# Second group of an FFN given three-pass products in its second layer, with late weight differences and one pair of attention blocks moved

## The chip, the cores and the metric

The kernel runs on one core of one Trainium2 chip. The metric is the device time of one execution in microseconds (us); the number to beat is the median of three timed runs, 521.12 us (521.03 to 521.21). A separate execution was profiled; its times are those of the profile below. The engines are called as the profile calls them: PE (matrix products), PEld (PE's loads of the stationary operand, which run beside its products), DVE (VectorE), ACT (ScalarE), POOL (GpSimd) and SP (SyncE, which only issues transfers here).

## The reference

The computation is gated linear attention followed by a two-layer FFN. All inputs are 64-bit floats on the host.

```
q, k, v: (4, 8, 768, 48)      alpha: (4, 8, 768, 48), between 0.8 and 1
for t in range(768):
    state = alpha[:, :, t, :, None] * state + einsum('bhd,bhe->bhde', k[:, :, t], v[:, :, t])
    y[:, :, t] = einsum('bhd,bhde->bhe', q[:, :, t], state)
x = y.transpose(0, 2, 1, 3).reshape(3072, 384)
h = maximum(x @ w_in, 0)           # w_in (384, 2048)
out = (h * h) @ w_out              # w_out (2048, 384)
```

The attention inputs reach the kernel as 32-bit floats. The weights reach it as 64-bit words, which DVE and ACT turn into fp32 by bit operations (`convert_first` to `convert_second`, from L154).

## The kernel before, in words

**Blocks and groups.** The sequence is cut into 6 chunks of 128 tokens. A chunk of one of the 4 batches is a block, so there are 24 blocks, and attention works on pairs of blocks (the pair that begins with block n is called pair n). Four blocks, 512 tokens, make a group of the FFN. There are 6 groups, 0 to 5 in the code; the text calls them group 0 to group 5, so "the second group" of the title is group 1 and "the third" is group 2. While the PE runs the FFN of one group, the attention of the next group's two pairs is worked in between.

**First layer.** The 2048 hidden rows are 16 tiles of 128 rows, two tiles to each of 8 pieces of the weights (a piece of `w_in` is 128x768 numbers, and so is a piece of `w_out`). A tile is 3 products of 128x128 by 128x512 per pass, since the model dimension is 3x128. The result is squared after a ReLU on ACT and DVE (`in_post`).

**Second layer.** Each hidden tile is multiplied, for each of the 4 token blocks t, with a 128x384 slice of `w_out`, and the 16 tiles are summed in one PSUM bank per block.

**Two ways to multiply.** A plain fp32 product (`out_plain`, `ffn_in`) is one matmul, which the trace shows as two records. The other way is three passes in a faster type (fp32r). The weight w becomes b, a rounded copy of 0.9998 w (`cast_w`, ACT), l, the rest w - b divided by 2^-12 (`rest_w` on DVE and `scale_w` on ACT), and d = b - l (`diff_w`, DVE). The data becomes a, l and d in the same manner (`split_to`, `diff_to`: a on ACT, l and d on DVE, once for each 128x512 tile). The product is (1 + E)(a b + l l) + d d with E = 2^-12. In the profile the passes carry the operands' names: `wb,xa`, `wl,xl`, `wd,xd` in the first layer, `wb,ha` (or `hx`), `wl,hl` (or `hx`), `wd,hd` in the second. `out_x` does the first two passes of a hidden tile, and `out_y` does the third afterwards, two pieces at a time.

**Which group uses which way.** Group 0: first layer plain; second layer plain for pieces 0 to 5 and three passes for 6 and 7 (`k0` = 2). Group 1: first layer in three passes; second layer plain for pieces 0 to 3 and three passes for 4 to 7 (`k1` = 4). Groups 2 to 5: everything in three passes.

**Where the parts live.** The parts are made once, by `prepare`, during groups 0 and 1. b stays in the core's memory. l and d are stored to DRAM as they are made (`keep`) and come back in each later group as that group needs them: `stream` puts their keys in the list `todo`, and `pump` (L699) issues the loads in that order while fewer than `room` buffers are in use; `used` frees a buffer after its last product and calls `pump`. In group 1 the parts needed in that group are kept instead of loaded (`diff_w`).

**What sets the order.** Each engine works its instructions in the order in which the program emits them. That order is written out: a layer is a list of units with a cost in PE time, and all the rest (attention, conversions, preparation, splits of x) are events with a time on the same scale. `weave` walks the units, adds up their costs and emits an event when the sum reaches its time. The table `AT` (L19) holds these times: `g1` and `g` say when the pairs of the next group begin, `g1x`, `gx` and `g0x` when the next group's x is split, `w_first`, `o0`, `o2` and `w_in_at` when parts of the weights are prepared. In `attention`, `joined`, `ga` and `gb` finish an older pair's outputs (with the copies `x<-y` at L628 that write the next group's x), and `turn` (matmuls at L590) transposes q and k of the pair that begins. SP issues all transfers in one order, and a transfer that has to wait (for instance a store of a part not yet made) holds all those behind it.

**Alignment.** `align` (L1016) asks for the PE's next instruction to lie at a given offset from a 256-byte boundary of the program. It is filled with empty instructions, which are the NOPs of L1018 in the profile. `places` and `pads` in `AT` say where. Before the change there are 5 such places, with 58, 26, 26, 26 and 22 NOPs.

**Lines of the profile.** L737 is the first layer's three passes, L930 the plain first layer, L820 every product of the second layer, L710 ACT's casts to a, L660 DVE's rests l and also `diff_w`'s and `in_y`'s sums, L714 DVE's differences d of the data, L754 and L752 ACT's work after the first layer, L628 the copies of y into x, L412 the matmuls of y, L490 the attention state's update.

## Time and profile before

| what | number |
|---|---|
| median of 3 runs | 521.12 us (521.03 to 521.21) |
| profiled execution | 521.61 us, of which the span that the trace covers is 519.8 us |
| busy: PE, PEld, DVE, ACT | 511.1, 421.5, 361.9, 316.4 us |
| granted PE clock | 1.00 in every stretch |
| plain products of the second layer (160 records), groups 0 and 1 | 53.5 us |
| third pass of the second layer (304) | 53.7 us |
| group 1, first product to group 2's first | 126.26 to 214.62 us |
| group 2, the same way | 214.62 to 295.75 us |

The span lacks the time around the execution: 521.61 - 519.8 = 1.8 us. The mean duration of a product overstates its cost, since products overlap at their ends; what one costs is found by dividing a stretch of back-to-back products by their number. Busy time of PE is near the whole span, so the profile has to be read by stretches of time, and by the idle time just ahead of a product, which the trace gives in square brackets together with what ended it.

### The profile page before, as it was taken

How to read it: one execution, taken by the hardware profiler on the slowest of the kernel's cores; microseconds unless marked ns; L12 is line 12 of the kernel's file. 1: busy time of each engine (PE TensorE's matmuls, PEld its weight loads, DVE VectorE, ACT ScalarE, POOL GpSimd, SP SyncE). 2: the span in 40 equal slices, each digit the busy share in tenths (PEclk: the TensorE clock that was granted, in tenths of full speed). 3: DMA queues.
4: the chain of work that ended last, by engine and by line, in shares of the span. 5: the costliest groups of instructions: out<-in, count | busy, mean ns of one | idle time of the engine just before them, and what ended most of it. 6: DMA issues, size and time to landing. Idle time of an engine off the chain costs nothing.

```text
span 519.8 us, 13204 instructions
## 1 busy us (share of the span) xinstructions
PE 511.1 (98%) x5350; PEld 421.5 (81%) x5350; DVE 361.9 (70%) x629; ACT 316.4 (61%) x664; POOL 5.4 (1%) x29
## 2 busy tenths in 40 slices
PE   8989999999999999999999999999999999999997
PEld 6775446668887669888899988899988899988997
DVE  3887969998979579757596466696465485363861
ACT  5678893687899566476963266962266863164620
POOL 4000000000000000000000000000000000000000
PEclk9999999999999999999999999999999999999999
DMA  9999686517878496998885796965684534798101
GB/s 182 210 262 262 178 216 172 75 51 240 243 228 200 117 280 161 272 338 234 201 235 156 242 269 185 231 172 162 217 269 124 183 123 153 254 355 295 68 0 62
DMA packets 139324, 102.36 MB, mean 197 GB/s; under 512 B 109808, under 2 KB 112896, under 8 KB 139264
## 3 DMA queue, kind: packets, MB, share of 16 engines
q1 hardware_dynamic: 139264, 101.52, 68.6%
q8 instruction: 43, 0.70, 0.6%
q14 instruction: 17, 0.14, 0.1%
HBM read 84.17 MB, written 17.33 MB: 195 GB/s over the span
## 4 chain that ended last, share of the span: by engine, by line
PE 93%; DVE 3%; DMA 1%; SPq 1%; issue 1%; ACT 0%; DVEq 0%; POOLq 0%
PE o L820 41%; PE h L737 32%; PE h L930 8%; PE y L412 4%; PE T L590 2%; PE sckv L432 2%; PE sckv L460 2%; DVE x L628 1%; DMA a_in<-in_alpha_dram 1%; PE cs L297 1%; SPq L344 1%; DMA last<-row 1%; PE cs L301 1%; PE cs L300 1%; SPq L119 0%
## 5 line engine op out<-in xcount | busy, mean ns | idle before, releaser
L737 PE MATMUL h<-xa,wb 128*128 128x512 f32 x240 | 69.2, 396 | 1.2 <-PE h L737 0.8
L737 PE MATMUL h<-xl,wl 128*128 128x512 f32 x240 | 68.1, 392 | 0.0
L737 PE MATMUL h<-xd,wd 128*128 128x512 f32 x240 | 66.6, 393 | 0.0
L754 ACT ACTIVATE h<-h 128x512 f32<-128x512 f32 x40 | 23.3, 581 | 57.9 <-PE h L737 57.7
L660 DVE TENSOR_TENSOR hid<-h,hid 128x512 f32<-128x512 f32 x40 | 27.5, 688 | 42.1 <-PE h L737 39.3
L628 ACT COPY x<-y 32x256 f32<-32x256 f32 (+2 forms) x132 | 47.2, 365 | 15.7 <-PE y L412 13.2
L820 PE MATMUL o<-wb,ha 128*128 128x384 f32 x160 | 54.2, 339 | 0.0
L820 PE MATMUL o<-wd,hd 128*128 128x384 f32 x304 | 53.7, 334 | 0.0
L820 PE MATMUL o<-w_out,hid 128*128 128x384 f32 x160 | 53.5, 490 | 0.0
L820 PE MATMUL o<-wl,hl 128*128 128x384 f32 x160 | 53.5, 334 | 0.0
L737 PEld LDWEIGHTS h<-xl,wl 128*128 128x128 f32 x240 | 44.9, 188 | 10.6 <-ACT wl L679 0.6
L737 PEld LDWEIGHTS h<-xa,wb 128*128 128x128 f32 x240 | 44.2, 188 | 11.1 <-PE h L737 1.2
L820 PEld LDWEIGHTS o<-wd,hd 128*128 128x128 f32 x304 | 52.8, 188 | 0.0
L737 PEld LDWEIGHTS h<-xd,wd 128*128 128x128 f32 x240 | 44.5, 188 | 9.2 <-ACT hid L752 0.2
L820 PE MATMUL o<-wb,hx 128*128 128x384 f32 x144 | 48.7, 338 | 0.0
L820 PE MATMUL o<-wl,hx 128*128 128x384 f32 x144 | 48.1, 334 | 0.0
L820 PEld LDWEIGHTS o<-w_out,hid 128*128 128x128 f32 x160 | 29.9, 190 | 19.7
L930 PE MATMUL h<-x,w_in 128*128 128x512 f32 (+1 forms) x120 | 43.0, 510 | 1.5 <-DVE s L489 1.2
L710 ACT ACTIVATE ha<-hid 128x512 fp32r<-128x512 f32 x40 | 25.4, 636 | 23.8 <-DVE hx L660 12.9
L752 ACT ACTIVATE hid<-h 128x512 f32<-128x512 f32 x40 | 24.3, 607 | 25.1 <-PE h L737 25.0
L930 PEld LDWEIGHTS h<-x,w_in 128*128 128x128 f32 x120 | 22.5, 190 | 18.6 <-issue 14.9
L660 DVE TENSOR_TENSOR hl<-hid,ha 128x512 fp32r<-128x512 f32 x40 | 27.4, 685 | 10.9 <-ACT ha L710 10.8
(115 smaller groups left out, 883.0 us busy)
## 6 DMA issues: line engine op xcount, KB each, us to landing
wd<-do SPq DMA_DIRECT2D x36, 384.0 KB
wl<-lo SPq DMA_DIRECT2D x34, 384.0 KB
wl<-li SPq DMA_DIRECT2D x32, 384.0 KB
wd<-di SPq DMA_DIRECT2D x32, 384.0 KB
raw<-in_moe_w_in_dram SPq DMA_DIRECT2D x8, 768.0 KB
raw<-in_moe_w_out_dram SPq DMA_DIRECT2D x8, 768.0 KB
v_in<-in_v_dram SPq DMA_DIRECT2D x24, 192.0 KB
out_dram<-osb SPq DMA_DIRECT2D x24, 192.0 KB
```

The source lines that it names most:

```text
L412: ins = nc.tensor.matmul(out=ys[e][64 * half : 64 * half + D + G * e, m % 2, p // 2, t], lhsT=lhsT, rhs=rhs, start=(half, e) not in seen, ...
L432: nc.tensor.matmul(out=ps[e][HALF[h], 0, p, :], lhsT=ks[rows, p, HALF[h]], rhs=qs[rows, p, HALF[h]], start=True, stop=True, skip_group_che ...
L460: nc.tensor.matmul(out=ps[h][64 * e : 64 * (e + 1), 1, p, G:64], lhsT=tile_of("k", n)[HALF[h], 2 * p + e, :], rhs=tiles["v"][n % NV][HALF[ ...
L590: nc.tensor.transpose(out=ps[h][:, i, p, :], in_=rows[HALF[h], 128 * p : 128 * (p + 1)], identity=ident[HALF[h], HALF[h]],)
L628: copy(out=x[kk][to : to + m, t : t + 2], in_=blk[n]["y"][e][r : r + m, :, p // 2],)
L660: nc.vector.tensor_tensor(out=o, in0=x, in1=z, op=op)
L710: nc.scalar.activation(out=a, in_=x, func=AF.Copy, scale=NEAR)
L737: nc.tensor.matmul(out=acc["h", j], lhsT=here[w, "i", p][:, kk, jj * 128 : (jj + 1) * 128], rhs=x_parts[x][:, kk], start=start and kk == 0 ...
L752: nc.scalar.activation(out=hid[j], in_=x, func=AF.Copy, scale=E)
L754: nc.scalar.activation(out=x, in_=x, func=AF.Copy, scale=1.0 + E)
L820: nc.tensor.matmul(out=acc[t][:, 0:DM], lhsT=lhs[:, t * C : (t + 1) * C], rhs=rhs, start=start, stop=stop, skip_group_check=True,)
L930: nc.tensor.matmul(out=ps, lhsT=w[:, kk, c0 : c0 + 128], rhs=xT[g][kk][:, cols], start=(kk == 0), stop=(kk == KM - 1),)
```

## The change

- Group 1 works all 8 pieces of the second layer in three passes. The plain path stays for group 0's six pieces only; `k1`, `h1`, `late`, `ffn_out` and `plain_out` go.
- Group 1 takes its pieces in the order 6, 7, 0, 1, 2, 3, 4, 5 in both layers (`pieces`, `tiles_of`, `js`), and `w_in`'s parts are prepared in that order. Group 0 already made the parts of pieces 6 and 7 of `w_out`.
- For the other six pieces of `w_out` (`lasting`), d is made late, all within a short stretch near the end of the second layer's first two passes (`d_at`, `d_by`), and it is written over l in l's own buffer (`here.pop` in `diff_w`). `used` therefore does not free such an l in group 1. The dict `made` goes; its entries are in `here`.
- Signs are turned round (-NEAR, and add in place of subtract). The products are the same: each has two negated factors or none.
- The tile splits at the start of a second layer begin one unit later in group 1 (`lead1` 5), and in every group the later splits are emitted up to 4 tiles ahead instead of 6 (`ahead`). The limit on buffers in group 1 is 23 instead of 22.
- In group 1 the third pair event no longer begins pair 12: it only finishes pair 10's outputs. Pair 12 begins in group 2, whose list `g2` has three entries and whose x splits have their own time (`g2x`).
- The loads of v and k in `attention` move (`v_by`), and so do many times in `AT`.
- `pads` has 11 entries instead of 3. With the two `places` that gives 13 alignments; their NOPs come to 288 instead of 158, by the addresses of the instructions.

In numbers of instructions emitted: PE matmuls 3683 to 3747 (32 plain ones go, 96 passes come), DVE tensor-tensor 347 to 355, DVE scalar-pointer forms 203 to 207, ACT activations 435 to 443, transfers 350 to 348.

The diff, cut; the table's entries are put one to a line:

```diff
 AT = {
-'v_by': (2.5, 3.5, 5.0)
+'v_by': (1.0, 0.87, 13.76)
-'pads': ((1, 33.0, 218), (2, 0.5, 83), (2, 5.5, 178))
+'pads': ((1, 20.0, 24), (1, 26.0, 232), (1, 33.0, 36), (1, 38.0, 111), (1, 43.0, 132),
+         (2, 2.0, 126), (2, 8.0, 248), (2, 13.0, 153), (2, 22.0, 42), (2, 28.0, 11), (2, 36.0, 72))
+'lead1': 5
-'w_first': (45.25, 42.0, 55.95)
+'w_first': (45.63, 40.88, 58.08)
+'d_at': 42.74, 'd_by': 0.4
-'w_late': 0.6, 'w_in_by': 3.4, 'room1': 22, 'ahead': 6
+'w_late': 2.1, 'w_in_by': 3.6, 'room1': 23, 'ahead': 4
-'g0': ((1.5, 4, False, True, 28.25), (20.25, 6, True, True), (28.75, 8, True, False))
+'g0': ((3.5, 4, False, True, 28.38), (21.25, 6, True, True), (27.13, 8, True, False))
-'g1': ((5.5, 8, False, 15.5), (15.5, 10, True), (34.5, 12, True))
+'g1': ((4.87, 8, False, True, 16.12), (15.49, 10, True, True), (32.99, 12, True, False))
+'g2': ((5.0, 12, False, True, 17.63), (15.63, 14, True, True), (35.0, 16, True, True))
-'g1x': 50.0, 'g0x': 55.25
+'g1x': 50.12, 'g2x': 49.99, 'g0x': 55.76
-'k1': 4, 'h1': 3
-'o0': (44.75, 47.25), 'o2': (21.75, 27.5, 31.75, 35.0, 41.25, 41.75), 'str1': 22.0
+'o0': (45.25, 46.87), 'o2': (20.75, 23.25, 27.62, 28.12, 32.24, 34.26), 'str1': 24.12
...
+    def lasting(w, p):
+        return w == "o" and p < NW - AT["k0"]
...
     def diff_w(w, p):
-        b, l = here["b", w, p].bitcast(FP32), made["l", w, p].bitcast(FP32)
-        d = made["d", w, p] = wt("wd", FP32R, shapes[w])
-        cut.add((w, p))
-        combine(((d, b, ALU.subtract, l),))
+        l = here["l", w, p]
+        d = here["d", w, p] = here.pop(("l", w, p)) if lasting(w, p) else wt("wd", FP32R, shapes[w])
+        combine(((d, here["b", w, p].bitcast(FP32), ALU.add, l.bitcast(FP32)),))
         keep("d", w, p)
...
     def pump():
-        while todo and todo[0] in stored and len(here) + len(made) + 2 * NW - len(cut) < room[0]:
+        while todo and todo[0] in stored and len(here) + 2 * NW - len(cut) < room[0]:
...
-    def used(*key):
-        here.pop(key)
+    def used(x, w, p):
+        if g_now[0] != 1 or x != "l" or not lasting(w, p):
+            here.pop((x, w, p))
         pump()
...
+    def pieces(g):
+        last = [*range(NW - AT["k0"], NW)]
+        return last if g == 0 else last + [*range(NW - AT["k0"])] if g == 1 else [*range(NW)]
+
+    def tiles_of(g):
+        return [2 * p + i for p in pieces(g) for i in range(2)]
...
     def layer_out(g):
-        plain = NW - AT["k0"] if g == 0 else NW - AT["k1"] if g == 1 else 0
+        ps, ns = pieces(g), tiles_of(g)
+        plain = NW - len(ps)
...
         if g == 1:
...
+            for i, at in enumerate(AT["o2"]):
+                events += prepare(
+                    at0 + at, "o", order[len(AT["o0"]) + i], 0, at0 + AT["d_at"] + AT["d_by"] * i
+                )
```

## The prediction

> **What bounds the kernel now.** I read first the busy times, then the chain of waits by engine, then a table of stages, then the idle time ahead of single products.

> ```profile
> PE 511.1 (98%) x5350; PEld 421.5 (81%) x5350; DVE 361.9 (70%) x629; ACT 316.4 (61%) x664; POOL 5.4 (1%) x29
> PE 93%; DVE 3%; DMA 1%; SPq 1%; issue 1%; ACT 0%; DVEq 0%; POOLq 0%
> 126.20:168.90 42.70, 42.70 (x506) 34.22 (x504) 37.64 (x68) 37.84 (x77) 0.00 (x0) 1.00 0.76 205
> 168.90:214.60 45.70, 45.70 (x556) 35.85 (x549) 36.13 (x65) 28.14 (x63) 0.00 (x0) 1.00 0.73 202
> 214.60:295.70 81.10, 79.91 (x923) 71.47 (x922) 52.97 (x100) 45.46 (x103) 0.00 (x0) 1.00 0.81 236
> ```

> PE is 98% busy and 93% of the chain: the number of products sets the time, and what else counts is what keeps PE waiting. The last three lines are stretches (length, then PE, PEld, DVE, ACT busy): both layers of group 1, then group 2. The clock is 1.00 in all. In group 1, DVE is at 37.64 of 42.70 and 36.13 of 45.70, 88% and 79%; in group 2 it is at 65%. So group 1, which the change makes shorter for PE and fuller for DVE, is where DVE is nearest to binding.

> ```profile
> 79.75 9.30 PE L820 MATMUL o<-w_out,hid 128*128 128x384 f32 x28
> 88.97 0.46 PE L590 MATMUL T<-ident,k_in 64*128 64x64 f32 x8
> 266.43 29.32 PE o L820 x168
> 126.26 1.08 PE L737 MATMUL h<-xa,wb 128*128 128x512 f32 x3
> 128.08 0.87 PE L737 MATMUL h<-xa,wb 128*128 128x512 f32 x3
> 216.97 0.93 PE L737 MATMUL h<-xa,wb 128*128 128x512 f32 x3 [0.81 <-PE h L737]
> 241.77 0.97 PE L737 MATMUL h<-xa,wb 128*128 128x512 f32 x3 [0.38 <-DVE hid L660]
> 148.57 0.96 DVE L660 TENSOR_TENSOR wd<-wb,wl 128x768 fp32r<-128x768 f32 x1 [2.46 <-ACT wl L679]
> 171.97 0.36 DVE L490 TENSOR_TENSOR s<-s,last 128x192 f32<-128x192 f32 x1 [2.82 <-DMA last<-row]
> L1018 PEldq NOP  x158: 13/13/13, 50.6 to 249.6; - x158
> ```

> Each timeline line is start, length, then what ran; brackets give idle time and releaser.

> **The products.** 28 records of plain products from 79.75 to the next kind at 88.97 take 9.22 us; a product is two records, so it costs 9.22/14 = 0.659. 168 three-pass products follow without a gap in 29.32: 0.1745 each, 0.5235 for three. The change swaps 32 of the first for 96 of the second: 32 x (0.659 - 0.5235) = **-4.3**.

> By the weight loads the sum would differ. PEld's loads of these products last 0.188 in the trace, more than the 0.1745 a product takes, so here they overlap one another. [...] If a three-pass product cost its load, 96 x 0.188 = 18.0 would replace 21.1, a gain of 3.0. The row of 168 back-to-back products decides for 0.1745.

> **Group 0 to group 1.** The first tile's six products take 126.26 to 128.08, 1.82, where six at the in-layer pitch of 0.227 take 1.36: a stall of 0.46 while the last splits of x arrive. The order of the instructions after the change puts y's second half and its copies into x earlier, so I take **-0.45** (between 0 and that).

> **Group 1, first layer.** Tiles are split into a, l and d; a tile's l and d cost DVE 0.685 + 0.692 by duration and about 1.32 back to back with their dependence. Three tiles' splits now lie here: +4.0 for DVE, and three casts of about 0.5, +1.6, for ACT. Lying in DVE's 5.1 idle us of the first stretch, they fit only if the idle time falls at the right places. Before points at which PE takes a buffer or an x cast just in time, the slack in the trace is 0.05 to 0.16 (at 144.50, 148.67, 156.24, 160.02, 161.72, 165.64). DVE's waits in group 1 up to 161 come to 3.8 (0.53, 0.38, 0.43, and the 2.46 shown); these can absorb most. I walked the new order by hand with the rows' pitches: **+1.6**. Bounds: 0 if all waits are absorbed, 3.8 if DVE's waits recur and all the added work is exposed.

> **Group 1, second layer.** The first half was plain and needed no splits; now all 16 tiles are split during it. Up to the last l, DVE has 9.66 us to do from the seventh tile's on, PE 8.33 until it needs it; the lead at the start covers part: **+0.95**, bounds 0 and 2.8 (the wait at 171.97 recurring in it). The six late d cost 6 x 0.87 = 5.2 of DVE (pitch of 128x768), but they end 3.5 to 6 us before the third pass reads them. They take 0 while that holds; if DVE is that much later, they are exposed one for one. Writing d over l makes each wait for l's last product, which is earlier by the order, and for the store of l, also earlier: 0. SP issues two transfers fewer: 0.

> **Group 1 to group 2.** The second tile waits: chain gap 0.80, idle 0.81 shown at 216.97, 0.98 with the pitch. It has two causes, l of the first `w_in` piece landing at about 215, which held PE's sequencer, and 26 NOPs just behind (215.04 to 216.92). That l now comes from the list earlier: **-0.98**. The casts and rests of x for group 2 are ordered later among the copies: +0.55 (bounds 0 and 0.98).

> **Group 2.** The stall of 0.58 at 241 ends a chain through `last<-row`, a transfer that holds DVE. It belongs to a pair's state update, which moves: **-0.58**. But two pairs and a begun third now lie in group 2: DVE has 28 us free there, so only the exposed ends count: **+0.3** (0 to 0.58, one more such chain).

> **Group 2 to group 3.** Pair 14's outputs now end 4.6 us before group 3's first product; 12 copies of y take 4.4 (line at 120.73 below), then come three casts and three rests of x. Between groups 0 and 1 that lead is 5.6 us and cost 0.46. One us less, of work which is serial on ACT and DVE: 0.46 + 1.0 = **+1.5**; 0.5 if the casts interleave with the copies, 2.0 at most by the walk.

> ```profile
> 120.73 4.37 ACT L628 COPY x<-y 32x256 f32<-32x256 f32 x12 [0.51 <-PE y L412]
> 125.12 1.67 ACT L710 ACTIVATE xa<-x 128x512 fp32r<-128x512 f32 x3
> 127.60 1.89 DVE L714 SCALAR_TENSOR_TENSOR xd<-xa,xl 128x512 fp32r<-128x512 f32 x3
> ```

> **The moved pair.** Pair 12's matmuls and copies on PE, about 4.5 us, leave group 1 and enter group 2: 0 on PE. `ahead` 4 emits splits two tiles later in groups 2 to 5; they still lead their products by four tiles of 1.4: 0, bounds -0.3 and +0.5. The new order of v and k loads puts k behind 13 us more: 0, as both are wanted a group later.

> **NOPs.** 26 take 1.88 us of the sequencer, 72 ns each; 130 more are 9.4 us. They cost when PE's queue runs dry, and the runs are of 8 to 44. Four of the five runs before have no gap behind them, and the fifth came after the sequencer had been held. I take 0; the other bound is +2.0, two or three 40-NOP runs (2.9 each) at places where the queue is short. [...]

> **Sum:** -4.3 - 0.45 + 1.6 + 0.95 - 0.98 + 0.55 - 0.58 + 0.3 + 1.5 = -1.4. The profiled execution would go from 521.61 (span 519.8 and 1.8 around it) to 520.2; it stands 0.5 above the median, so on the median 521.12 - 1.4 = **519.7**.

> **The rivals.**
> - *Waits are hidden.* DVE's own waits of 3.8 in group 1 absorb the splits: 521.12 - 4.3 - 0.45 - 0.98 - 0.58 + 1.5 + 0.3 = 516.6. For it: DVE has 5.1 and 9.6 idle us in the two stretches. Against: the small slacks. Chance 0.20.
> - *DVE becomes the bound of group 1* (the other side). By the walk the last split comes 0.5 us late with no idle time on DVE at all, so every microsecond that DVE idles between 126 and 190 passes to PE; the forecast's 1.6 + 0.95 = 2.55 is that 0.5 and 2.05 of idle time. If the waits of before recur, 3.8 and some two fifths of the 2.8 (1.15, the state update being ordered among the last splits), PE loses 0.5 + 4.95 = 5.45, 2.9 more than forecast: 519.7 + 2.9 = 522.6. The change stops gaining from 2.05 + 1.4 = 3.5 us of idle time. For it: 88% and 79% busy with more work in less time, and waits on ACT and on a transfer that nothing in the diff takes away. Against: the state update begins at another time. Chance 0.20.
> - *Handoffs and NOPs eat the gain.* Group 2 to 3 at 2.0, xl at 0.98, one NOP run exposed: 519.7 + 0.5 + 0.43 + 0.5 = 521.1. Chance 0.14.
> - *The loads set the pitch.* The gain of 3.0 in place of 4.3: 519.7 + 1.3 = 521.0. Chance 0.04.

> **How the numbers follow.** The forecast, 519.7, has 0.42 with its own range 518.4 to 520.9. This kernel's runs differ by 0.03%; 0.2%, 1.04 us, is about what a measurement can tell from no change: faster is below 520.08, slower above 522.16. Faster: 0.30 of the forecast's 0.42 and 0.20 of hidden waits, 0.50. Same: the other 0.12, 0.14 and 0.04, and a little of DVE's case, less 0.02 for its tail, 0.28. Slower: DVE's case and that tail, 0.22. The range reaches from the hidden waits to DVE's case, 516.8 to 522.6.

> **What would show it.** After: no `w_out,hid` records past group 0, so 96 records and not 160; `wd,hd` 336. Group 1's second layer without its plain half, the whole group about 81.7 us with pair 12's 4.5 gone (88.4 - 4.3 - 4.5 - 0.45 + 2.55), group 2 near 84.9 (81.1 + 4.5 - 0.98 + 0.55 - 0.58 + 0.3). If waits are right, idle time ahead of `h` products in group 1 released by DVE `hid` or `hl`, 1 to 3 us; if DVE binds, more than 4 us ahead of `ha`, `hl` products with DVE over 95% there. The idle time at the first tile of group 3 should be 1 to 2 us, released by DVE `xl`. An idle time behind `NOP` runs would falsify their 0. A three-pass product off 0.1745 in group 1, or idle time ahead of `wd` products, falsifies the first term or the late differences' cover.

## The result and the profile after

The changed kernel takes 526.99 us (526.55 to 527.69, four runs) against 521.16 (521.03 to 521.81): the ratio is 1.011, with a 95% interval of 1.0093 to 1.0128. The forecast was 519.7, the range 516.8 to 522.6. The profiled execution of the changed kernel took 527.69, with a span of 525.2 against 519.8.

These are the busy times and the chain by engine of the changed kernel, and its stages: both layers of group 1, then groups 2 and 3. A stage line has its length, then the busy time of PE, PEld, DVE and ACT.

```profile
PE 513.2 (98%) x5382; PEld 426.4 (81%) x5382; DVE 370.8 (71%) x641; ACT 319.8 (61%) x672; POOL 5.4 (1%) x29
PE 83%; DVE 7%; ACT 6%; DMA 2%; issue 1%; SPq 0%; POOL 0%; DVEq 0%; ACTq 0%; POOLq 0%
```

```profile
126.60:170.70 44.10, 43.45 (x506) 34.52 (x504) 40.43 (x72) 38.43 (x78) 0.00 (x0) 1.00 0.76 205
170.70:210.00 39.30, 38.48 (x426) 36.71 (x418) 30.44 (x50) 25.55 (x54) 0.00 (x0) 1.00 0.65 212
210.00:299.50 89.50, 86.28 (x1086) 74.66 (x1084) 59.78 (x116) 48.85 (x116) 0.00 (x0) 1.00 0.75 208
299.50:380.30 80.80, 80.60 (x889) 71.36 (x890) 54.94 (x100) 46.23 (x105) 0.00 (x0) 1.00 0.74 210
```

PE's share of the chain has fallen from 93% to 83%, and DVE and ACT together have risen to 13%. Group 1 has become shorter (83.4 us, from 88.4) and group 2 much longer (89.5, from 81.1). The profile says 98% for PE in both kernels. The share of busy time hides what happened, because a product that starts late is drawn long (0.44 us at 188.54 below, where its neighbours take 0.33).

So I set PE's time against its work. Each product gets the pitch at which such products run back to back in the trace (0.1735 to 0.1745 for one of the second layer's passes, 0.2267 for one of the first's, 0.664 for a plain one); what a step from one product to the next takes beyond that is a gap. Gaps above 0.16 us are listed by themselves, and the smaller ones are summed.

| us | before: work, small, listed | after: work, small, listed | difference |
|---|---|---|---|
| up to group 1 | 126.26 | 126.62 | +0.36 |
| group 1 | 85.84, 2.22, 0.29 | 77.41, 3.18, 2.81 | -8.43 +0.96 +2.52 |
| group 2 | 77.41, 2.01, 1.56 | 81.28, 3.27, 4.96 | +3.87 +1.26 +3.40 |
| group 3 | 76.92, 2.30, 0.17 | 76.92, 2.51, 1.31 | +0.21 +1.14 |
| groups 4 and 5 | | | 0.0 |

The work is down by 8.43 - 3.87 = 4.56 us, and the gaps are up by 9.5. That makes +5.3, of the 5.4 by which the spans differ. How much of it is work hangs on the pitch of a plain product. The 64 records that go from group 1 took 20.74 us in three stretches of the kernel before (5.36, 10.13 and 5.25), 0.648 a product and not 0.664; with that the work falls by 4.05 and the small gaps grow by 1.9 in place of 2.43. Of this growth, 1.3 us lie in the steps right behind a listed gap; what the rest is was not worked out. The largest gaps are in group 2. Here are PE's products around two of them, and the NOP runs of the same stretch and of one that follows (number, then first and last start).

```profile
211.19 1.10 PE L741 MATMUL h<-xl,wl 128*128 128x512 f32 x2
212.12 0.86 PE L741 MATMUL h<-xa,wb 128*128 128x512 f32 x3
214.73 0.93 PE L741 MATMUL h<-xa,wb 128*128 128x512 f32 x3 [1.05 <-issue]
224.87 0.93 PE L741 MATMUL h<-xa,wb 128*128 128x512 f32 x3 [0.98 <-ACT inv L312]
232.86 0.93 PE L741 MATMUL h<-xa,wb 128*128 128x512 f32 x3 [0.21 <-issue]
```

```profile
L1003 PEldq NOP  x40: 13/13/13, 211.8 to 214.7; - x40
L1003 PEldq NOP  x40: 13/13/13, 221.9 to 224.8; - x40
L1003 PEldq NOP  x40: 13/13/13, 229.8 to 232.8; - x40
L1003 PEldq NOP  x10: 13/13/13, 259.5 to 260.1; - x10
```

Each of the four gaps (1.22, 1.15, 0.38, and 0.31 at 260.20; 3.06 in all) ends 0.07 us after the last NOP of a run, to the hundredth: 214.66 and 214.73, 224.80 and 224.87, 232.79 and 232.86, 260.13 and 260.20. In the second, the view of waits names ACT, which is only the last semaphore that it sees. The gap of 0.98 in the kernel before also ends so, 216.91 and 216.97.

The other gaps are waits for data. The timeline shows one of the four in group 1's first layer that end with ACT's scaled l of `w_in`, two in its second layer, released by DVE, and the start of group 3, released by the casts and rests of x.

```profile
150.07 0.97 PE L741 MATMUL h<-xl,wl 128*128 128x512 f32 x3 [0.21 <-ACT wl L685]
188.54 0.44 PE L833 MATMUL o<-wl,hx 128*128 128x384 f32 x1 [0.28 <-DVE hx L660]
192.21 0.45 PE L833 MATMUL o<-wl,hx 128*128 128x384 f32 x1 [0.54 <-DVE hx L660]
299.54 1.55 PE L741 MATMUL h<-xa,wb 128*128 128x512 f32 x3 [0.53 <-ACT xa L714]
300.92 1.51 PE L741 MATMUL h<-xl,wl 128*128 128x512 f32 x3
```

### The profile page after: what moved, and what is told of

Read it like the earlier page. It is cut to its first block, busy times and chain, and to the rows that moved or that the text cites. A ratio compares the mean times of both kernels' runs of the same rounds, so it can differ in the third digit from the quotient of the medians.

```text
span 525.2 us, 13413 instructions
## 1 busy us (share of the span) xinstructions
PE 513.2 (98%) x5382; PEld 426.4 (81%) x5382; DVE 370.8 (71%) x641; ACT 319.8 (61%) x672; POOL 5.4 (1%) x29
## 4 chain that ended last, share of the span: by engine, by line
PE 83%; DVE 7%; ACT 6%; DMA 2%; issue 1%; SPq 0%; POOL 0%; DVEq 0%; ACTq 0%; POOLq 0%
PE o L833 34%; PE h L741 28%; PE h L933 7%; PE y L412 4%; PE sckv L432 2%; PE T L590 2%; ACT x L628 2%; DVE hd L718 2%; PE sckv L460 2%; DMA raw<-in_moe_w_in_dram 1%; ACT wl L685 1%; PE cs L297 1%; DVE hx L660 1%; PE warm L251 1%; DVE xl L660 1%
## 5 line engine op out<-in xcount | busy, mean ns | idle before, releaser
L628 ACT COPY x<-y 32x256 f32<-32x256 f32 (+2 forms) x132 | 46.9, 366 | 38.2 <-PE y L412 35.8
L833 PE MATMUL o<-wb,ha 128*128 128x384 f32 x176 | 59.4, 338 | 0.0
L833 PE MATMUL o<-wl,hl 128*128 128x384 f32 x176 | 58.9, 335 | 0.0
L660 DVE TENSOR_TENSOR hid<-h,hid 128x512 f32<-128x512 f32 x40 | 27.5, 688 | 41.9 <-PE h L741 35.9
L833 PE MATMUL o<-wl,hx 128*128 128x384 f32 x160 | 53.9, 337 | 0.8 <-DVE hx L660 0.8
L833 PE MATMUL o<-wb,hx 128*128 128x384 f32 x160 | 54.0, 338 | 0.1
L833 PE MATMUL o<-wd,hd 128*128 128x384 f32 x288 | 51.7, 336 | 0.0
L833 PEld LDWEIGHTS o<-wd,hd 128*128 128x128 f32 x288 | 49.8, 188 | 0.3
L660 DVE TENSOR_TENSOR hl<-hid,ha 128x512 fp32r<-128x512 f32 x44 | 30.2, 686 | 15.3 <-ACT ha L714 15.2
L660 DVE TENSOR_TENSOR osb<-o,osb 128x384 f32<-128x384 f32 x24 | 12.7, 551 | 30.3 <-PE o L833 22.7
L714 ACT ACTIVATE ha<-hid 128x512 fp32r<-128x512 f32 x44 | 27.5, 630 | 10.1 <-PE o L833 5.6
L833 PEld LDWEIGHTS o<-wb,ha 128*128 128x128 f32 x176 | 33.0, 188 | 0.4
```

The source lines that it names most:

```text
L628: copy(out=x[kk][to : to + m, t : t + 2], in_=blk[n]["y"][e][r : r + m, :, p // 2],)
L660: nc.vector.tensor_tensor(out=o, in0=x, in1=z, op=op)
L714: nc.scalar.activation(out=a, in_=x, func=AF.Copy, scale=-NEAR)
L833: nc.tensor.matmul(out=acc[t][:, 0:DM], lhsT=lhs[:, t * C : (t + 1) * C], rhs=rhs, start=start, stop=stop, skip_group_check=True,)
```

## The experiments

There were seventeen runs of kernels, in five sets. Times of one set are compared with the kernel before on the same chip, whose median was 521.3 to 521.9. "The gap" of a run is always the listed kind, above 0.16 us.

### Alignments and their NOPs

**All alignments left out of the changed kernel.**

```diff
-'places': ((4, 202), (16, 141)), 'pads': ((1, 20.0, 24), ... (2, 36.0, 72))
+'places': (), 'pads': ()
```

> The changed kernel with all 13 alignments and their 288 NOPs left out; the order of the work is the same. Theory N (a run of NOPs costs PE when the sequencer comes to it with little queued): the four gaps behind NOP runs in the changed kernel's trace, 1.22, 1.15, 0.38 and 0.31, go, 3.06 in all, so about 524.0 (from 526.99). Rival A (at the second gap the release by ACT's inv, 0.16 before the NOPs end, would hold PE anyway, and at the first a transfer): 1.0 to 2.0 of it stays, 525 to 526. Rival L (the alignment of the following code is worth something by itself): no gain or a loss, 527 or more.

Measured: 524.42, ratio 1.0055 (1.0038 to 1.0073). The four gaps are gone and group 2 takes 86.61 instead of 89.51; groups 1 and 3 are as they were (83.45 and 80.75). Theory N holds to 0.4 us. The rest, 2.8 us of span above the kernel before, is there without any NOP. The trace puts all its listed gaps past group 0, but one of 0.17, down to data and none to a program block (these blocks come with the next runs). So in this order the alignments bought nothing and cost 2.6 us by the medians.

**Only the three runs of 40 left out**, the other runs' lengths kept.

```diff
-'places': ((4, 202), (16, 141)), 'pads': (... (2, 2.0, 126), (2, 8.0, 248), (2, 13.0, 153), (2, 22.0, 42), (2, 28.0, 11), (2, 36.0, 72))
+'places': ((4, 202), (16, 21)), 'pads': (... (2, 22.0, 178), (2, 28.0, 147), (2, 36.0, 208))
```

> The changed kernel without the three runs of 40 NOPs in group 2's first layer; the other ten runs keep their counts. Theory N: the gaps at 214.73, 224.87 and 232.86 go, 1.22 + 1.15 + 0.38 = 2.75, so 524.2, and nearly all of what leaving out every run gives. Rival A: the gap at 224.87 stays at about 1.0, 525.2. Rival L: 527 or more.

Measured: 527.21, ratio 1.0105 (1.0074 to 1.0135). The three gaps are gone, at 224.87 too, so rival A falls. But the time did not move: new gaps of 0.76, 0.56, 0.66 and 0.61 stand at 288.57, 319.06, 346.47 and 399.95, where there had been none. So rival L has something too.

**All alignments left out of the kernel before.**

```diff
-'places': ((4, 203), (16, 188)), 'pads': ((1, 33.0, 218), (2, 0.5, 83), (2, 5.5, 178))
+'places': (), 'pads': ()
```

> The kernel before without its five alignments (158 NOPs). Theory N: only the gap of 0.98 behind the NOPs at 216.91 goes, 520.2. Rival A, as the prediction had it in part: that gap is the late transfer of l and stays, 521.1. Rival L: slower than 521.2.

Measured: 524.98, ratio 1.0066 (1.0044 to 1.0088); its profiled execution took 526.8. So the five alignments were worth 3.6 us to the kernel before, against every theory but L. In its timeline, one gap stands in the middle of a tile's three products, and no data is named:

```profile
237.64 0.84 PE L737 MATMUL h<-xd,wd 128*128 128x512 f32 x3
238.32 0.39 PE L737 MATMUL h<-xa,wb 128*128 128x512 f32 x1
240.30 0.62 PE L737 MATMUL h<-xa,wb 128*128 128x512 f32 x2 [1.58 <-issue]
```

The trace also has 42 to 44 packets of 16384 bytes in a queue that the profile names `instruction` (`q8`). One starts at 237.51 and lands at 238.97, 1.33 us before the gap's end. The same holds of the new gaps of the runs above: each ends 1.27 to 1.49 us after such a packet landed. I then counted PE's instructions from the program's start (weight loads, semaphore instructions and NOPs with them) up to each of these gaps. The counts are 5631, 7425, 8191 and 9216 here, and 6912, 7681, 8447 and 9472 in the run without the three 40s: all multiples of 256, give or take one. The totals fit as well: the trace of the kernel before has 10998 records of PE instructions, 42.96 times 256, and 43 such packets; that of the changed kernel has 11200, 43.75 times 256, and 44. At 16384 bytes a block, that is 64 bytes an instruction. So the boundary from which `align` counts must be one of 256 instructions: a boundary of 256 bytes would be four instructions away at most, and in the next run the fill is 128 NOPs.

**A shift by half a block** in the kernel before.

```diff
-'places': ((4, 203), (16, 188)), 'pads': ((1, 33.0, 218), (2, 0.5, 83), (2, 5.5, 178))
+'places': ((4, 17),), 'pads': ()        # one run of 128 NOPs, in group 0
```

> The kernel before with a single run of 128 NOPs, in group 0's plain part, in place of its five runs. The run itself is hidden there if 9.2 us of backlog exist, else it costs up to 4. Theory F (what the alignments set is where the 16 KB blocks in which PE's program is fetched begin, 256 instructions each; a block that begins in a dense stretch of small products arrives late): against the kernel before without alignments, the gaps at 240, 318, 344 and 399 move by half a block to other instructions; each costs 0.5 to 1.8. Rival P (the gaps belong to those instructions, which wait for something): they stay where they are.

Measured: 528.26, ratio 1.0125 (1.0097 to 1.0152). Groups 2 to 4, which had 5.6 us of gaps without alignments, now have one of 0.18. Two new gaps of 2.10 and 1.79 stand in group 1 at instructions 4097 and 4864, both in the small products of y. Behind the first the granted clock falls (0.59 in the stage line below), and six plain products take 1.8 us longer. Group 1 starts 2.3 us later, probably by the 128 NOPs ahead of it. Theory F holds: the gaps belong to the blocks and not to the instructions.

```profile
170.82 0.58 PE L412 MATMUL y<-am,v_in 64*48 64x64 f32 x23
173.30 0.33 PE L412 MATMUL y<-am,v_in 64*48 64x64 f32 x3 [1.91 <-issue]
```

```profile
173.30:177.50 4.20, 4.20 (x10) 2.45 (x10) 2.76 (x5) 0.00 (x0) 0.00 (x0) 0.59 0.61 151
```

Over nine kernels, past 60 us, I worked out the products' time within the block ahead of each boundary. Of the fifteen boundaries where it was under 2.5 us, ten had a gap, of 0.4 to 3.7 (at one of them, 344.56 in the kernel before without alignments, DVE's d came at the same time); four of the other five lie at 101 to 103 us. Between 2.5 and 4.4 us it was mixed: three of seven had a gap, among them the one shown at 240.30. Where it was 4.4 us or more, gaps that nothing else explains were rare: 0.19 once, and 0.28 to 0.52 at instruction 4607 in three other runs. I read this so: a block with little work, most of all one that is dense with the small products of attention, can be used up before the next one is there. Ahead of the product at 240.30, PE's last one had ended at 238.71 and the packet landed at 238.97; what fills the 1.33 us from there on was not shown. In the kernel before and in the changed one, the alignments leave no block under 4.4 us.

**A dose of NOPs** in the kernel before, in groups 4 and 5. It asks for PE's reserve: how long PE can go on with what the sequencer has already given it when the sequencer comes to a run.

```diff
-'pads': ((1, 33.0, 218), (2, 0.5, 83), (2, 5.5, 178))
+'pads': (... (4, 12.0, 214), (4, 20.0, 254), (4, 40.0, 47), (4, 48.0, 209),
+         (5, 6.0, 107), (5, 14.0, 4), (5, 36.0, 81), (5, 44.0, 17))
```

> The kernel before with eight more runs of NOPs: 20, 40, 20, 40 in group 4 (first layer, then second) and 40, 60, 40, 60 in group 5, at 72 ns each. [...] If the reserve is smaller than a run, gaps show behind the runs of 40 and 60 and each run costs the same beyond it: 2.9 and 4.3 less the reserve; with no reserve at all the sum of 320 NOPs, 23 us.

Measured: 523.9 in a single run, span 522.1. In group 4 the runs of 40 leave no gap at all. In group 5 the gaps are 0, 0.29, 0.21 and 1.47 behind 40, 60, 40 and 60. Of 320 NOPs, 23 us of the sequencer, PE saw 2.0 us. And in this run the 26 NOPs at group 2's start, 214.0 to 215.8, leave no gap: the l of `w_in` ahead of them landed at 213.8 in place of 214.9, while PE still had products of group 1 to work.

```profile
L1018 PEldq NOP  x40: 13/13/13, 404.1 to 406.9; - x40
L1018 PEldq NOP  x60: 13/13/13, 464.5 to 468.8; - x60
L1018 PEldq NOP  x60: 13/13/13, 505.6 to 510.0; - x60
```

A run's length less its gap is the lead that the sequencer had over PE when it came to the run: 4.0 us at 464.5, 2.9 at 505.6, over 2.9 at 404.1, but 1.6 in the changed kernel at 211.8 and 0.9 in the kernel before at 215.0. At 211.80 the run of 40 begins within 0.01 us of PE's return from a wait for l of x (211.79): the sequencer had been waiting too. Where nothing seems to have held it, the lead is 16 to 18 products whatever their length: 4.0 / 0.227 in the first layer, 2.9 / 0.1735 and 2.7 / 0.1735 in the second (the last for the 40 NOPs with a gap of 0.21). This is an estimate from the three gaps of this one run.

**The run of 26 at group 2's start moved**, first into the last products of group 1, then behind three tiles of group 2.

```diff
-'pads': ((1, 33.0, 218), (2, 0.5, 83), (2, 5.5, 178))
+'pads': ((1, 33.0, 218), (1, 51.5, 29), (2, 5.5, 178))      # the first kernel
+'pads': ((1, 33.0, 218), (2, 3.5, 114), (2, 8.0, 203))      # the second
```

> The kernel before, with the run of 26 NOPs that stands at the start of group 2 moved into the end of group 1's second layer, where a queue of 0.17 us products stands ahead of it. All other runs keep their counts and all later blocks their places. Theory N: the gap of 0.98 at 216.97 goes, and the time is 0.2 to 1.0 below the kernel before on the same chip (in one run of the same instructions that gap was absent already). Rival: the gap is the transfer of l, it stays, no change.

> The kernel before with the run of 26 NOPs of group 2's start put at 3.5 instead of 0.5, and the run at 5.5 put at 8.0, so that each stands behind some tiles that waited for nothing. Theory N (the place counts): both runs leave no gap, the 0.98 goes, 0.3 to 1.0 below the kernel before on the same chip. Rival (26 NOPs cost near 0.7 to 1.0 wherever the first layer's products are short): no change, or slower by up to 1.

Measured: 521.52, ratio 0.9996 (0.9987 to 1.0006), with a gap of 0.68 behind the moved run; and 522.42, ratio 1.0018 (1.0005 to 1.0030), with 1.13 behind it, while the run moved to 8.0 left none. The same 26 NOPs cost 0 to 1.13 by their place. My rule for a good place (some undisturbed products ahead) did not find one; the sequencer's lead was 1.3 and 0.7 us at these two. In the second, a semaphore instruction of PE's sequencer stands at 219.62, 0.13 before the run's first NOP, and two semaphores that it waits for were raised at 219.59 and 219.61, so a wait had just held it. What held it in the first stays open.

### Pair 12 and the third pass

**Pair 12 back in group 1**, without alignments.

```diff
-'g1': (... (32.99, 12, True, False))
-'g2': ((5.0, 12, False, True, 17.63), (15.63, 14, True, True), (35.0, 16, True, True)), 'g2x': 49.99
+'g1': (... (32.99, 12, True, True))
+'g2': ((1.7, 14, True, True), (15.5, 16, True, True)), 'g2x': 48.25
```

> The changed kernel without alignments and with pair 12 begun in group 1 again, as before; group 2 gets the standard two events and x splits at 48.25. To be compared with the changed kernel without alignments (524.42). Theory H (the late end of pair 14 before group 3 is what the move costs): the stall at group 3's start goes, about 2.0, and group 1 grows by no more than the pair's 4.2 on PE, which group 2 loses: 522.4. Theory D (in group 1 DVE and ACT have no room for the pair's work besides the splits of 16 tiles): group 1's gaps, 2.8 now, grow by 3 to 6, and the time is 525.5 to 528.

Measured: 527.91, ratio 1.0128 (1.0096 to 1.0159). Group 3 has no gap now (79.35), so its stall is a product of the move. Group 1 has 5.58 of gaps in place of 2.82; the new ones, 1.33, 0.41, 0.52 and 1.28 between 188 and 197, are waits for DVE by `cs`, a split and the transposes. In that part theory D is right. But group 2 has a block gap of 3.67 at instruction 5633 and one of 0.67 at 6399, which no theory had, and 2.4 us more behind the first, in which products take 0.2 to 0.36 longer each. The timeline shows the first gap, and in the stretch behind it the granted clock (the number behind POOL's 0.00) was 0.52:

```profile
240.27 0.92 PE L412 MATMUL y<-am,v_in 64*64 64x64 f32 x25 [3.47 <-issue]
```

```profile
240.20:245.80 5.60, 5.53 (x36) 4.41 (x36) 0.96 (x2) 0.58 (x1) 0.00 (x0) 0.52 0.82 248
```

**The same with the blocks placed** (three runs of 24 NOPs), **and with the pair begun at 36.**

```diff
-'g1': (... (32.99, 12, True, True)), 'pads': ()
+'g1': (... (32.99, 12, True, True)), 'pads': ((1, 45.0, 29), (1, 52.0, 91), (2, 22.0, 254))
+'g1': (... (32.99, 12, True, False), (36.0, 12, False, True))      # the second kernel, 24, 24 and 16 NOPs
```

> The changed kernel with pair 12 begun at 33 in group 1 again and group 2 as before, with three runs of 24 NOPs that keep every later block of 256 instructions at 4.6 us of products or more. The same order without them took 527.91 with two block gaps of 3.67 and 0.67 and about 2.8 of slowed products behind the first. Theory F (those were the blocks' places alone): they go, 520.7 to 521.3, so moving the pair costs about 3. Rival (group 2's start holds PE there anyway): 523 or more, and the move costs nothing.

> As pair_back_pads, but pair 12 begins three units later (36), apart from pair 10's finish (33). With it at 33 PE waited 1.33, 0.41, 0.52 and 1.28 for DVE at 188 to 197, at 40 it waited 1.85 for ACT at 208 and 0.84 at group 2's start. Theory D (DVE is full until the last split at 192 and has room behind): those waits shrink to about 1, 519 to 520. Rival (the waits move along with the pair, whatever its place): within 0.7 of pair_back_pads.

Measured: 527.63, ratio 1.0123 (1.0099 to 1.0148), and 528.09, ratio 1.0127 (1.0103 to 1.0151). The block gaps are gone, as theory F said, but each of the three runs of NOPs left a gap of its own: 0.65, 1.56 and 1.50 in the first kernel. The second of them follows a wait for l of x, as in the changed kernel, and slows eight products behind it.

```profile
L1003 PEldq NOP  x24: 13/13/13, 219.3 to 221.0; - x24
```

```profile
218.66 1.10 PE L741 MATMUL h<-xl,wl 128*128 128x512 f32 x2
221.04 1.00 PE L741 MATMUL h<-xa,wb 128*128 128x512 f32 x3 [1.29 <-issue]
```

```profile
221.00:225.50 4.50, 4.46 (x13) 3.53 (x14) 2.13 (x5) 0.81 (x2) 0.00 (x0) 0.62 1.03 334
```

So these two did not settle what the move costs. Taking the block gaps and the slowed products out of the first run's trace (527.9 - 3.67 - 0.67 - 2.4) leaves a span of about 521.2, 1.4 below the changed kernel without alignments. That is an estimate, and no run shows it. With the pair begun at 36, the waits of group 1 are 0.45, 0.96, 0.41 and 1.20 in place of the four, and one of 0.77 in place of 0.24 at group 2's start: they moved along with the pair, for the greater part.

**Pair 12 begun at 40**, with runs of 48, 0, 20 and 10 NOPs.

```diff
+'g1': (... (32.99, 12, True, False), (40.0, 12, False, True))      # g2 and g2x as with the pair back
```

> The changed kernel with pair 12 begun in group 1 after all, but late, at 40 (after the splits, beside the third pass), group 2 with the standard events and x splits at 48.25, and four runs of NOPs (48, 0, 20 and 10) that keep every block of 256 instructions at 4.4 us of products or more. Theory D: DVE has room there, so neither the 3.3 us of waits at 188 to 197 that pair 12 had when begun at 33, nor the 2.1 at group 3's start come back: from the 520.7 that the run with the pair back would have without its block gaps, less 2 to 3: 517.5 to 519. Rival: the late start meets the late differences and x's copies, and group 2 begins late: 520 to 523.

Measured: 524.43, ratio 1.0062 (1.0040 to 1.0084). The time is above even the rival's: the transposes wait 1.85 for ACT's copies at 208.50, the granted clock behind that wait is 0.50 until 212.6, which costs 1.8, and group 2's first tiles wait 0.84 and 0.37 for l of x. None of the three places tried in group 1 takes the pair without a wait.

**One more piece in three passes**, in the kernel before.

```diff
-'k1': 4
+'k1': 5
```

> The kernel before with one more piece of group 1's second layer in three passes: 5 of 8 in place of 4, everything else, alignments too, as before. Theory of the products: 8 plain products become 24 passes, 8 x 0.1355 = 1.08 less on PE, 520.1 if the two more tiles' splits (2.6 us of DVE) find room. If DVE already binds at that point: the splits cost up to 2.6, and the time is 521.1 to 522.7.

Measured: 526.21, ratio 1.0089 (1.0056 to 1.0121), against 521.87. The products' work falls by 1.14 at the pitches of the table, 1.0 at 0.648 a plain product. Group 1 nevertheless takes 94.07 in place of 88.35: its transposes wait 1.83 and 1.59 for DVE's scaled k and q at 194.85 and 197.66. Two more tiles' splits are 2.6 us of DVE. They cost PE 3.8 in waits of the transposes, and behind these the granted clock was 0.50 from 196.2 to 202.9, which cost 2.6 more; a block gap of 0.40 at 208.53 came in as well. With pair 12 in place, DVE had too little room just there. From 190 to 199 it is busy 8.65 of 9.00 us here and 6.26 in the kernel before; the first line is this run:

```profile
190.00:199.00 9.00, 5.92 (x53) 5.07 (x52) 8.65 (x15) 5.39 (x14) 0.00 (x0) 0.84 0.33 88
190.00:199.00 9.00, 9.00 (x147) 7.47 (x149) 6.26 (x11) 7.99 (x19) 0.00 (x0) 1.00 0.86 202
```

### Which waits hold group 1

**DVE's differences of 12 hidden tiles left out** (the third pass then multiplies zeros there).

```diff
+        if g_now[0] == 1 and n < 12:
+            nc.gpsimd.memset(h_diff[n].bitcast(FP32), 0.0)
+            return
         diff_to(h_diff[n], *h_parts[n])
```

> The changed kernel without alignments, leaving out DVE's difference d of 12 of group 1's hidden tiles (8.3 us of DVE; POOL writes zeros there instead, so that part of the second layer's third pass is left out of the result). To be compared with 524.42. Theory D (in group 1's second layer DVE is the bound): the gaps at 188.8 and 192.5, 0.47 and 0.70, go with their restarts, 1.4 in all: 523.0. Rival (ACT's casts or the buffers hold those products): the gaps stay, 524.4.

Measured: 524.12, ratio 1.0037 (1.0023 to 1.0052), against 1.0055 with them. Group 1 takes 81.92 instead of 83.45, 1.53 less: the gaps at 188.8 and 192.5 are gone with their restarts. Theory D is right for the second layer, in size too, while the medians, from different chips, show less than 1.4.

**Seven eighths of ACT's scaling of w_in's rests left out** (the second pass of the first layer then has wrong weights).

```diff
-        nc.scalar.activation(out=l, in_=l.bitcast(FP32), func=AF.Copy, scale=1.0 / E)
+        z = l[:, :, 0:32] if w == "i" else l
+        nc.scalar.activation(out=z, in_=z.bitcast(FP32), func=AF.Copy, scale=1.0 / E)
```

> The changed kernel without alignments, scaling only an eighth of each l of w_in (ACT's 0.75 us becomes some 0.2, for eight pieces; the first layer's second pass is left with wrong weights in the rest). To be compared with 524.42. Theory A1 (in group 1's first layer ACT is the bound, and PE waits for scaled l and for its casts): the gaps at 134.6, 144.0, 145.0, 150.3, 157.0 and 162.2, 1.65 with about 0.9 of restarts, go: 521.9. Rival D1 (DVE's rests and the squares behind them hold the same products): half or more of it stays, 523.3 or more.

Measured: 524.78, ratio 1.0053 (1.0035 to 1.0072). Group 1 takes 83.07, 0.4 less. Of the six gaps, 1.65 together, five are gone, among them all four that the trace puts down to ACT's scaled l. One of 0.29 at 144.2 stays, and three that were not there, 0.25 at 155.85 and 0.19 and 0.20 at 163, stand at other products; a block gap of 0.35 came in at 198.16. So ACT's scaling is what those four waits ended with. But more than half of the 1.65 comes back as waits for other data (where the trace names one, it is DVE's scaled k or q, or an earlier product of h), which is what rival D1 says.

### The end of pair 14

**Group 2's third event at 29; then split, pair 14 finishing at 33 or 30 and pair 16 beginning at 38.** All are without NOPs (the second has `'pads': ((1, 45.0, 56), (2, 22.0, 40), (2, 36.0, 50))`, which came to none).

```diff
-'g2': (... (35.0, 16, True, True)), 'g2x': 49.99
+'g2': (... (29.0, 16, True, True)), 'g2x': 48.25                               # the first kernel
+'g2': (... (33.0, 16, True, False), (38.0, 16, False, True)), 'g2x': 48.25     # the second
+'g2': (... (30.0, 16, True, False), (38.0, 16, False, True)), 'g2x': 48.25     # the third
```

> The changed kernel without alignments, with the third attention event of group 2 at 29 in place of 35 and the x splits of group 3 at 48.25 in place of 49.99. To be compared with 524.42. Theory H: pair 14's outputs end some 6 us earlier, the copies into x are done before group 3 begins, and its first tile has no stall: 0.68 + 1.16 + about 0.3 of restarts go, 522.3. Rival: the same work on ACT and DVE then meets the splits of the second layer, new gaps of the same size appear there, 524 or more.

> The changed kernel without alignments, group 2's third event split: pair 14 finishes two units earlier (33), pair 16 begins three later (38), x splits at 48.25. To be compared with 524.42; no block has under 3.7 us. Theory H: the stall at group 3's start (0.68 + 1.3 with restarts) shrinks by the 2.8 us gained, to under 0.3, and no wait replaces it, since pair 16's begin no longer meets the splits: 522.4. Rival (as with the whole event at 29, where 2.9 came in elsewhere): 524 or more.

> As finish_14_33, with pair 14's finish at 30. Theory H: the stall at group 3's start is gone, 522.2 to 522.5, no better than at 33. Rival: the copies of y into x, 4.4 us on ACT, delay the casts of group 2's last tiles, and a gap of 1 or more comes in the second layer: 523.5 or more.

Measured: 524.78 (1.0055, 1.0035 to 1.0075), 524.39 (1.0062, 1.0045 to 1.0080) and 524.10 (1.0068, 1.0043 to 1.0092), no better than 524.42. In all three the stall at group 3's start is gone, and group 3 takes 79.4 to 79.5. In all three group 2 takes 1.0 to 2.2 more, with waits that were not there: 1.59 by the transposes for DVE's q at 272.61 in the first, with 1.7 more behind it, where the granted clock was 0.50 until 276.5; 1.20 for ACT's copies at 285.77 in the second, which also has a block gap of 0.52 in group 1; 0.54, 0.94 and 0.74 in the last:

```profile
279.87 0.96 PE L833 MATMUL o<-wd,hd 128*128 128x384 f32 x4 [0.37 <-ACT osb L874]
285.15 0.27 PE L590 MATMUL T<-ident,k_in 64*128 64x64 f32 x1 [0.76 <-ACT x L628]
285.93 0.46 PE L590 MATMUL T<-ident,k_in 64*128 64x64 f32 x7 [0.51 <-ACT x L628]
```

Theory H is right on where the stall comes from and wrong on what it is worth: wherever pair 14's finish was put, about one microsecond or more came back as other waits for DVE and ACT.

## Why the prediction was wrong

- **The products, -4.3.** Right to 0.3 us: 20.74 less 96 passes at 0.1735 to 0.1745 is 4.0 to 4.1. The plain pitch of 0.659, read in group 0, is a little long for group 1. Pair 12's share only changes groups. The weight loads, 0.188 each, set no pitch; the passes ran at 0.1735 to 0.1745 in the undisturbed stretches.
- **Group 0 to group 1, -0.45.** Right: the first six products have no gap. Group 1 starts 0.36 later all the same; this start lay between 126.1 and 127.4 in the kernels without long NOP runs in group 0, so nothing is concluded from it.
- **Waits in group 1, +1.6 and +0.95.** The listed gaps are 1.65 in the first layer and 1.15 in the second. Both sizes were right. In the second layer so was the cause: the run without the differences shows DVE. In the first layer the size was right in part by luck. The prediction counted DVE's added splits and looked for products of h released by DVE's `hid` or `hl`; the trace names ACT at all six gaps, at four of them the scaled l of `w_in`, and the run without the scaling removes these four but leaves other waits.
- **What was left out of every wait.** A product behind a wait is often followed by another step that is 0.11 too long, for instance at 134.71, 150.40 and 192.49. Over groups 1 to 3 the small gaps grew by 1.9, of which 1.3 lie in such steps. The prediction put this at nothing: by the 0.11, ten waits of 0.3 would cost some 4 us and not 3, an estimate.
- **Group 1 to group 2, -0.98 and +0.55.** The second is right: 0.61 for l of x. The first named both causes, a hold by the transfer of l and the NOPs behind it, and the dose run bears it out: with l 1.1 us earlier the same NOPs left no gap. What failed is that taking the hold away would end it. Behind group 1 there now stand 40 NOPs behind another hold, for l of x, with a gap of 1.22.
- **NOPs, 0 with a bound of +2.0.** This is the step that failed: 3.06 in the trace, and 2.6 in the medians without them. It is the largest step and not the only one, since without any NOP the time, 524.42, is still above the range. The 0 rested on an estimate of PE's reserve that no run shows, and the trace before had one run out of five that went wrong. The reserve that the runs show is 16 to 18 products, 2.7 to 4.0 us, where nothing holds the sequencer (an estimate from the dose run), and 0.2 to 1.7 us at most of the runs that left gaps; at three of these a wait of the sequencer had just ended.
- **What the NOPs are for** was not in the prediction at all. It weighed them as a cost only. In the kernel before they keep 256-instruction blocks out of dense stretches, worth 3.6 us. An edit to PE's program moves the blocks, as the 128 NOPs did, so this has to be looked at anew, and it can come out the other way: in the changed kernel the blocks leave no gap without any alignment, and leaving out three runs of thirteen brought four gaps in. Without any alignment the two kernels are 524.98 and 524.42.
- **Group 2, -0.58 and +0.3.** The wait for the transfer is gone; the new ones, 0.40 at `cs` and 0.19 at a transpose, are 0.3 more than taken.
- **Group 2 to group 3, +1.5.** 1.84 in listed gaps (0.70, 0.30, 0.29, 0.18, 0.37), all but one released by ACT's casts and DVE's rests behind the copies of y (at one the trace names a load of v). The mechanism was right, and the size near the upper bound of 2.0.
- **The rivals.** DVE as the bound of group 1, 522.6, is the nearest in kind. It took hold in another form: without moving the pair DVE would have held PE more (3.8 us of waits in the run with one more piece), and the move turned this into waits at the other end of group 2. "Handoffs and NOPs eat the gain" named the right two, and bounded the second too low: +0.5, against 3.06.

In all: 3.06 for NOPs, 2.4 for small gaps (1.9, and the 0.45 of group 1's start that lay among them before), 0.36 at the start, 0.3 each for group 2, its end and the products turn the forecast of -1.4 into +5.3 or so. Settled are the products, the NOPs, the blocks and DVE in group 1's second layer. Open are what would hold the first layer without ACT's scaling, what the small gaps are apart from the 1.3, and what moving the pair costs by itself. No version beat the kernel before; the nearest was the one with the moved run, at 0.9996.

## What to carry to other kernels

In these kernels the gaps of the blocks stood at multiples of 256 PE instructions, and 128 NOPs took 5.4 us of them out of groups 2 to 4 and put 3.9 us into group 1. So where an edit adds or removes PE instructions, count the instructions from the program's start and look at what lies in each block, before and after, as one looks at buffers. Align only where a trace without alignments shows a gap: the alignments were worth 3.6 us in the kernel before and cost 2.6 in the changed one. Price a run of empty instructions by the lead that the sequencer has there, at most 16 to 18 products in these runs (an estimate) and 0.2 to 1.7 us at most of those that left gaps. With DVE 88% and 79% busy in group 1's two layers, work moved out of that group was not free: group 3's start took 1.84 us of gaps. Look where the moved work's copies will stand next, add to each new wait the slow step behind it (0.11 us here), and look at the granted clock behind a long wait (0.50 behind waits of 1.3 to 3.5 us in seven executions here).
